# A list scheduler that fixes the order of all operations, with zero-padded keys and natural token order, in a kernel of attention and a dense layer

## The chip, the cores and the metric

One core of one Trainium2 chip. The metric is device time in microseconds (us). The kernel before takes 255.26 us, the median of 2 runs (254.85 to 255.68). All runs below have one core; an execution over 1.5% above the fastest of its kernel is set aside as slow.

Engines are named as in the profile: PE (TensorE matmuls), PEld (TensorE weight loads), DVE (VectorE), ACT (ScalarE), POOL (GpSimd), SP (SyncE, which issues the loads and stores). SBUF and PSUM are the two on-chip memories in which the kernels place their tiles; here every matmul writes to PSUM.

## The reference

Four batches, eight heads, 768 tokens, head size 64. Retrieval heads see the causal half of the scores. Streaming heads see four sink tokens and a window of 64. Which head is which is data. A dense layer with a maximum of two projections follows.

```python
scores = scale * np.matmul(q, k.transpose(0, 1, 3, 2))       # (4, 8, 768, 768)
stream_keep = causal & (is_sink | in_win)                    # n_sink 4, window 64
mask = np.where(is_retrieval_of_head, full_mask, stream_mask)
a = softmax(np.where(mask, scores, -1e9))
x = np.matmul(a, v).transpose(0, 2, 1, 3).reshape(3072, 512)
h1 = x @ w1                                                  # (3072, 1024)
h2 = x @ w2
out = np.maximum(h1, h2) @ w_out                             # (3072, 512)
```

Both kernels use max(h1, h2) = h2 + relu(h1 - h2). So w1 - w2 is prepared once ("wd"), and w2 @ w_out once ("merge", wm). Per token block remain the *up* matmuls (x @ wd, then relu) and the *down* matmuls (x @ wm + relu(...) @ w_out).

## The kernel before

It works through 16 pairs of heads. A pair is loaded, cast to bfloat16 on POOL, transposed on PE, scored, exponentiated on ACT, multiplied by masks on DVE in the near blocks, multiplied by v on PE, and normalised on DVE. The dense work of batch b-1 is sprinkled between the attention steps of batch b by quotas. The framework's scheduler makes the final order.

The two heads of a pair lie one above the other in partitions, so each score matmul uses 64 rows of the array, and the two heads run side by side:

```python
for (j, q0, w, off) in segs:
    for hh in range(2):
        nc.tensor.matmul(sc[hh][:, off:off + w],
            lhsT=kt[64 * hh:64 * hh + 64, j * 128:(j + 1) * 128],
            rhs=qt[64 * hh:64 * hh + 64, q0:q0 + w],
            start=True, stop=True, skip_group_check=True)
```

q and k are loaded in packets of two tokens (512 bytes), which leaves even and odd tokens apart, and the copies after the transposes put them back in order with strides:

```python
in_=src[b, h0:h0 + 2].rearrange("h (m p r) d -> p h m (r d)", p=128, r=2)    # load of q, k
...
o = t.rearrange("q (m p r) -> q m r p", p=128, r=2)
i = psb[:, 0:S].rearrange("q (m r p) -> q m r p", p=128, r=2)
if which == 0: nc.vector.tensor_copy(out=o, in_=i)      # qt
else:          nc.scalar.copy(out=o, in_=i)             # kt
```

All 24 mask tiles are built on DVE before anything else:

```python
for h in range(H):
    for m in range(3):
        nc.vector.scalar_tensor_tensor(out=msk[:, h, m, :], in0=(far0 if m == 0 else far),
            scalar=nsf[:, h:h + 1], in1=causal, op0=ALU.mult, op1=ALU.add)
```

The quota that mixes dense work (`fill`) into attention (`seq`):

```python
quota = total / left / (len(seq) + 2)
...
for si, f in enumerate(seq):
    f()
    ...                      # transposes of the next pair at steps 6 and 8
    spend(quota)             # emits dense steps from fill
```

The softmax here doesn't subtract the row's maximum and nothing guards it: scores larger than these inputs give would overflow.

## Time and profile before

| | before |
|---|---|
| timed, median | 255.26 us |
| span of the profile | 252.9 us |
| PE, DVE, ACT, POOL busy | 84, 59, 50, 22% |
| first score matmul starts | 21.84 us |
| first up matmul starts | 79.89 us |

Lines of the profile page of the kernel before: busy time of each engine (share of the span, instructions), then the span in 40 slices of 6.3 us, each digit the busy share in tenths; PEclk is the granted clock of TensorE.

```profile
PE 212.4 (84%) x1869; PEld 111.9 (44%) x1888; DVE 150.1 (59%) x323; ACT 127.7 (50%) x233; POOL 54.9 (22%) x72
...
PE   0304992649898999999999999999999999999993
...
DVE  6997459864767663675478428546754675370520
ACT  2104880015777675676577666666676667401001
...
PEclk9999999999999999999999999999999999999999
```

PE is at 8 and 9 tenths from the 10th slice (57 us) on, and mostly idle or patchy before that. DVE and ACT are never full for long. The windows view gives the same in us (stretch; length; busy us and instructions of PE, PEld, DVE, ACT, POOL; granted clock; DMA share; GB/s):

```profile
0.00:40.00 40.00, 18.19 (x150) 9.80 (x150) 29.11 (x70) 15.70 (x27) 12.33 (x20) 1.00 1.02 292
40.00:60.00 20.00, 11.31 (x65) 6.48 (x66) 14.70 (x20) 1.96 (x3) 12.65 (x7) 1.00 1.12 243
60.00:100.00 40.00, 37.49 (x388) 20.69 (x390) 25.62 (x55) 27.66 (x53) 9.43 (x14) 1.00 0.44 111
100.00:150.00 50.00, 48.64 (x463) 25.35 (x468) 29.87 (x68) 31.96 (x59) 11.52 (x18) 1.00 0.43 121
150.00:200.00 50.00, 48.45 (x467) 25.29 (x472) 29.15 (x66) 33.42 (x62) 8.95 (x14) 1.00 0.13 44
```

PE is busy 37.5 of 40 us from 60 to 100 us and 97% after that, and the first 60 us hold 29.5 us of PE. So PE binds from 80 us at the latest, where the dense work starts. But "busy" is not "at its peak": a matmul's record runs past the start of the next. The distance from start to start is the better measure. Here is the PE timeline (start us, us, line, operation, output<-inputs, count):

```profile
128.32 0.81 PE L306 MATMUL h<-xt,wd_bf 128*128 128x384 bf16 x4
128.98 0.30 PE L232 MATMUL po<-vb,at 128*128 128x65 bf16 x4
...
130.44 0.81 PE L306 MATMUL h<-xt,wd_bf 128*128 128x384 bf16 x4
131.18 0.39 PE L209 MATMUL sc<-qt,kt 64*128 64x384 bf16 x4
```

Four up matmuls followed by a value matmul take 128.98 - 128.32 = 0.66 us, 165 ns each. Four up matmuls followed by a score take 131.18 - 130.44 = 0.74 us. The median of the interval is 162 ns between up matmuls, and 258 ns from an up matmul to a score: 96 ns are lost where the array changes from 128 to 64 rows.

The chain of waits at the start (start us, us, what):

```profile
5.98 9.44 DVE msk L122 x16
...
16.32 3.86 DVE msk L122 x8
20.18 0.71 DVE bias_94 L126
20.89 0.92 DVE qt L186
...
21.84 1.05 PE sc L209 x6
```

DVE built masks for 14 us, and the copy of the first queries stood behind them in its queue. The first score had to wait for that copy.

### The profile page before, as it was taken

How to read it: one execution, taken by the hardware profiler on the slowest of the kernel's cores; microseconds unless marked ns; L12 is line 12 of the kernel's file. 1: busy time of each engine (PE TensorE's matmuls, PEld its weight loads, DVE VectorE, ACT ScalarE, POOL GpSimd, SP SyncE). 2: the span in 40 equal slices, each digit the busy share in tenths (PEclk: the TensorE clock that was granted, in tenths of full speed). 3: DMA queues.
4: the chain of work that ended last, by engine and by line, in shares of the span. 5: the costliest groups of instructions: out<-in, count | busy, mean ns of one | idle time of the engine just before them, and what ended most of it. 6: DMA issues, size and time to landing. Idle time of an engine off the chain costs nothing.

```text
span 252.9 us, 4818 instructions
## 1 busy us (share of the span) xinstructions
PE 212.4 (84%) x1869; PEld 111.9 (44%) x1888; DVE 150.1 (59%) x323; ACT 127.7 (50%) x233; POOL 54.9 (22%) x72
## 2 busy tenths in 40 slices
PE   0304992649898999999999999999999999999993
PEld 0202551524454644465455545554555464454541
DVE  6997459864767663675478428546754675370520
ACT  2104880015777675676577666666676667401001
POOL 0741119930412213041303121212220100000000
PEclk9999999999999999999999999999999999999999
DMA  5999999993084365535544322012002101111212
GB/s 140 247 268 336 359 399 256 269 254 93 1 189 94 95 166 175 160 89 145 167 106 135 96 81 66 0 44 84 3 0 76 51 3 43 44 41 41 83 44 83
DMA packets 55639, 31.78 MB, mean 126 GB/s; under 512 B 25920, under 2 KB 50496, under 8 KB 55616
## 3 DMA queue, kind: packets, MB, share of 16 engines
q1 hardware_dynamic: 55472, 31.46, 45.4%
q8 instruction: 15, 0.25, 0.4%
q14 instruction: 8, 0.07, 0.1%
q10 hardware_dynamic: 144, 0.01, 0.0%
HBM read 25.17 MB, written 6.29 MB: 124 GB/s over the span
## 4 chain that ended last, share of the span: by engine, by line
PE 67%; DVE 22%; ACT 5%; issue 3%; DMA 2%; ACTq 0%
PE h L306 17%; PE y L320 15%; PE po L232 11%; PE sc L209 9%; DVE msk L122 5%; PE y L317 5%; DVE at L222 4%; PE tp L181 4%; PE wmp L156 3%; DVE x L275 3%; ACT at L218 3%; PE xtp L284 3%; DVE wo_bf L141 2%; DVE w_bf L138 2%; DMA ir_raw<-in_is_retrieval_dram 2%
## 5 line engine op out<-in xcount | busy, mean ns | idle before, releaser
L218 ACT ACTIVATE at<-sc 128x512 bf16<-128x512 f32 (+1 forms) x96 | 48.9, 565 | 24.7 <-PE sc L209 24.5
L222 DVE TENSOR_TENSOR at<-at,msk 128x512 bf16<-128x512 bf16 (+1 forms) x96 | 39.5, 426 | 21.7 <-ACT at L218 21.2
L209 PE MATMUL sc<-qt,kt 64*128 64x256 bf16 (+3 forms) x320 | 42.2, 300 | 10.8 <-DVE qt L186 9.4
L306 PE MATMUL h<-xt,wd_bf 128*128 128x384 bf16 x256 | 50.8, 326 | 0.5 <-ACT ot L323 0.3
L232 PE MATMUL po<-vb,at 128*128 128x65 bf16 x672 | 46.5, 201 | 4.1 <-DVE at L222 2.6
L320 PE MATMUL y<-wo_bf,gt 128*128 128x512 bf16 x190 | 47.7, 379 | 0.1
L232 PEld LDWEIGHTS <-at 128*128 128x128 bf16 x672 | 33.3, 101 | 32.2 <-DVE at L222 15.4
L309 DVE TENSOR_SCALAR gt<-h 128x384 bf16<-128x384 f32 x64 | 35.1, 554 | 20.0 <-PE h L306 18.6
L323 ACT COPY ot<-y 128x512 f32<-128x512 f32 x24 | 14.0, 585 | 54.7 <-PE y L320 54.7
L218 ACT ACTIVATE at<-sc,bias_j 128x512 bf16<-128x512 f32 (+1 forms) x64 | 34.2, 588 | 10.7 <-PE sc L209 10.6
L188 ACT COPY kt<-tp 128x768 bf16<-128x768 bf16 x16 | 16.4, 1026 | 30.7 <-PE tp L181 30.7
L169 POOL CAST qb<-qn 128x768 bf16<-128x768 f32 x16 | 14.1, 883 | 72.4 <-issue 55.4
L306 PEld LDWEIGHTS <-wd_bf 128*128 128x128 bf16 x256 | 22.7, 97 | 15.5 <-issue 3.3
L209 PEld LDWEIGHTS <-kt 64*128 64x128 bf16 x320 | 12.9, 96 | 30.4 <-issue 24.6
L320 PEld LDWEIGHTS <-gt 128*128 128x128 bf16 x192 | 18.0, 98 | 18.4
L317 PE MATMUL y<-wm_bf,xt 128*128 128x512 bf16 x82 | 24.8, 380 | 0.7
L169 POOL CAST kb<-kn 128x768 bf16<-128x768 f32 x16 | 14.2, 888 | 35.5 <-PE tp L181 30.7
L172 POOL CAST vb<-vn 128x768 bf16<-128x768 f32 x16 | 13.8, 863 | 34.4 <-issue 16.7
L218 ACT ACTIVATE at<-sc,bias_94 128x512 bf16<-128x512 f32 x32 | 20.3, 693 | 0.1
L286 DVE COPY xt<-xtp 128x768 bf16<-128x768 bf16 x16 | 8.9, 558 | 18.7 <-PE xtp L284 18.7
L186 DVE COPY qt<-tp 128x768 bf16<-128x768 bf16 x16 | 16.2, 1018 | 3.3 <-PE tp L181 2.9
L181 PE MATMUL tp<-ident,qb 128*128 128x128 bf16 x96 | 9.8, 236 | 9.5 <-POOL qb L169 9.4
(38 smaller groups left out, 140.7 us busy)
## 6 DMA issues: line engine op xcount, KB each, us to landing
qn<-in_q_dram SPq DMA_DIRECT2D x16, 384.0 KB, 6.1
kn<-in_k_dram SPq DMA_DIRECT2D x16, 384.0 KB, 5.3
vn<-in_v_dram SPq DMA_DIRECT2D x16, 384.0 KB, 5.2
out_dram<-ot SPq DMA_DIRECT2D x24, 256.0 KB, 2.0
w_182<-in_moe_w_dram SPq DMA_DIRECT2D x1, 2048.0 KB, 10.3
wo<-in_moe_w_out_dram SPq DMA_DIRECT2D x1, 2048.0 KB, 14.0
w_186<-in_moe_w_dram SPq DMA_DIRECT2D x1, 2048.0 KB, 19.1
ir_raw<-in_is_retrieval_dram ACTq DMA_DIRECT2D x1, 8.0 KB, 4.3
```

Source lines behind the costliest of these rows:

```text
L169: nc.gpsimd.tensor_copy(out=t.rearrange("p n h d -> p h n d"), in_=src.rearrange("p h m (r d) -> p h (m r) d", d=D))
L181: nc.tensor.transpose(psb[:, n * 128:(n + 1) * 128], src[:, n].rearrange("p h d -> p (h d)"), ident)
L186: nc.vector.tensor_copy(out=o, in_=i)
L188: nc.scalar.copy(out=o, in_=i)
L209: nc.tensor.matmul(sc[hh][:, off:off + w], lhsT=kt[64 * hh:64 * hh + 64, j * 128:(j + 1) * 128], rhs=qt[64 * hh:64 * hh + 64, q0:q0 + w], ...
L218: nc.scalar.activation(out=at[:, 0:n], in_=sc[hh][:, 0:n], func=ACT.Exp, scale=scale, bias=bias)
L222: nc.vector.tensor_mul(out=at[:, 0:n], in0=at[:, 0:n], in1=mk)
L232: nc.tensor.matmul(po[hh][:, i * (D + 1):(i + 1) * (D + 1)], lhsT=at[:, off + t * 128:off + (t + 1) * 128], rhs=vb[:, hh, j, :], start=(st ...
L306: nc.tensor.matmul(ps[:, 0:GT], lhsT=wd_bf[:, c, f * 128:(f + 1) * 128], rhs=xts[b][:, c, g * GT:(g + 1) * GT], start=(c == 0), stop=(c == ...
L309: nc.vector.tensor_relu(out=gts[g][:, f, :], in_=ps[:, 0:GT])
L317: nc.tensor.matmul(ps, lhsT=xts[b][:, c, c0:c0 + 128], rhs=wm_bf[:, c, :], start=(c == 0), stop=False)
L320: nc.tensor.matmul(ps, lhsT=gts[g][:, f, t * 128:(t + 1) * 128], rhs=wo_bf[:, f, :], start=False, stop=(f == FC - 1))
```

## The change

Its intent: plan the order of all operations inside the kernel, instead of sprinkling dense work by quotas. Every step becomes an operation with a modelled cost for each engine that may do it, its dependencies, its buffers and a priority. A list scheduler picks, at each step, the operation that can start earliest. This fixes order, engine and buffers. Attention has the lower priority number, so dense work fills what it leaves. Besides:

- each head is scored alone; its keys are padded with 64 zero rows, so every score uses all 128 rows and PE never changes mode;
- q and k come in natural token order, in 256-byte packets, and the copies become plain;
- relu, the output copy and the transposed copies may go to ACT or DVE;
- the mask has two tiles for each head instead of three; weights come in four pieces each; input buffers hold three pairs.

The core of the diff, with cuts:

```diff
+class Plan:
+    def schedule(self):
+        ...
+        while todo:
+            best = None
+            for e, lst in ready.items():          # PE, ACT, DVE, POOL, SP
+                pick = None
+                for o in lst:
+                    t = open_at(o)                # inputs ready and a buffer free
+                    if t is None: continue
+                    s = max(t, clock[e])
+                    key = (s, o.prio) if s > clock[e] + 1e-9 else (clock[e], o.prio)
+                    ...
+            o.engine, o.start, o.end = e, s, s + o.cost[e]
+            ...
+            o.done = o.end + LAT[e]               # PE 0.26, ACT 0.18, DVE 0.17
...
-                nc.tensor.matmul(
-                    sc[hh][:, off:off + w],
-                    lhsT=kt[64 * hh:64 * hh + 64, j * 128:(j + 1) * 128],
-                    rhs=qt[64 * hh:64 * hh + 64, q0:q0 + w],
+                        nc.tensor.matmul(sc.t[:, off:off + w], lhsT=kz.t[:, hh, j * 128:(j + 1) * 128],
+                                         rhs=qt.t[:, q0:q0 + w], ...)
+                o = P.op(score, {"PE": sum(s[2] for s in segs) / 2400 + 0.003 * len(segs)}, tops,
+                         [qt, kz, sc], prio=hr + 0.1 * st)
...
-                out=t, in_=src[b, h0:h0 + 2].rearrange("h (m p r) d -> p h m (r d)", p=128, r=2))
+                out=t.t, in_=src[b, h0:h0 + 2].rearrange("h (n p) d -> p h n d", p=128)),
...
-                nc.vector.tensor_relu(out=gts[g][:, f, :], in_=ps[:, 0:GT])
+                ups.append(P.op(relu, {"DVE": 0.467, "ACT": 0.37}, [o], [bk, gt], prio=15 + b))
...
+    order = P.schedule()
+    with tc.manual_schedule():                    # the framework keeps this order
+        for o in order:
+            o.emit(o.engine)
```

## The prediction

> **What bounds the kernel now.** TensorE. The windows view has PE busy 23.3 to 23.4 of every 24 us from 80 to 200 us and 13.85 of 14 to 214 us; DVE and ACT are near 60% there. Busy is not peak: the starts of successive matmuls in the timeline (80 to 214 us) give 162 ns for an up matmul (128x384), 216 ns for a down matmul (128x512), 56 ns for a transpose, about 29 ns for a value matmul (128x65) at best but 41 ns on average. At the best rates this window's work is about 108 us; it took 134.
>
> The first 80 us are worse: the first score starts at 21.84 us (behind 14 us of mask building in the chain of waits), PE works 2.5 of the first 21 us, and until about 57 us transposes come 107 ns apart, half the later rate, although the page shows the clock granted in full.
>
> **What the change does.**
> 1. Scores. Two heads now run side by side on 64 rows each. Padded, they run one after the other: 86,016 columns at 2.4 per ns is 36 us instead of 18: +18 us of PE.
> 2. No switch of array mode. The Trainium skill (TensorEngine Tiling, Tiling Modes, Key Properties) says that a mode switch drains the array. This trace agrees: up followed by a score takes 258 ns instead of 162, down followed by a score 312 instead of 216. The PE order of before has 200 such switches: 200 x 95 ns = -19 us. So 1 and 2 cancel.
> 3. Startup. The mask no longer delays qt, and the qt/kt copies (1018 and 1026 ns, strided) become plain ones (like xt, 558 ns). All input packets shrink to 256 bytes; at 20 to 22 ns a packet on 16 queues that is about 0.2 MB/us, so q and k of pair 0 land near 6.5 us and the first score starts near 10 us, not 22. Three pairs, the weights and the fourth pair (11 MB) land by about 41 us; dense work of batch 0 starts near 48 us instead of 80.
> 4. Balance. Relu, ot and the copies go to either of ACT and DVE; together they have about 230 us, so neither binds. Attention runs first; the PE order leaves some 68 us of pure dense work for the end, which packs well (97% in before's 214 to 250 us).
>
> **Sum.** PE work at best rates: up 41.5, down 62.2, merge 6.9, transposes 17.9, value 20.5, scores 36.6: 186 us. By 48 us about 28 us of it are done. The middle (90 us of work, static order, three score banks, waits on exp and mask) at about 90% takes 99 us; the dense end takes 70 us; the last copy and store 3 us. 48 + 99 + 70 + 3 = 220 us span; the timed run was 2.4 us over the span. I take a little off for overlap.
>
> **Prediction:** 219 us, 208 to 232. Faster by over 2%: 0.97; within 2%: 0.02; slower: 0.01.
>
> **What would show it.** First score near 10 us; up matmuls from about 48 us; no score followed by a gap of 95 ns; 512-column scores 216 ns apart; ACT and DVE both 50 to 65%; a dense end of about 70 us; transposes 56 ns apart before 57 us.
>
> **What would make it wrong.** PE staying at half rate through the startup (then +8 us); the 256-byte loads starving pair 3 so that the fixed order stalls; waits of value matmuls on masks, since the order is fixed by modelled durations; on the good side, a middle packed above 95% (-6 us).

## The result, and the profile after

The changed kernel takes 223.89 us (223.88 and 223.90, 2 runs). Ratios in this document are the mean time of one kernel's fast runs over that of the other's of the same rounds, so not quite the ratio of the quoted medians: 0.8766 here, 95% interval 0.8727 to 0.8805. That is within the predicted 208 to 232 us, 4.9 us above the point.

| | before | after |
|---|---|---|
| timed, median | 255.26 us | 223.89 us |
| span of the profile | 252.9 us | 221.9 us |
| PE, DVE, ACT, POOL busy | 84, 59, 50, 22% | 90, 55, 68, 22% |
| first score | 21.84 us | 13.60 us |
| first up matmul | 79.89 us | 53.65 us |
| last value matmul | 219.3 us | 146.7 us |

The same lines of the page and of the windows view, for the changed kernel:

```profile
PE 199.0 (90%) x1888; PEld 125.7 (57%) x1888; DVE 122.7 (55%) x298; ACT 151.2 (68%) x291; POOL 48.9 (22%) x59
...
PE   0267986799999999999999999999999999999993
...
DVE  6978999993799888988986876730000000000000
ACT  2158997675988989999989999933527253352721
...
PEclk9999999799999999999999999999999999999999
```

```profile
0.00:40.00 40.00, 23.25 (x284) 16.29 (x284) 36.05 (x86) 24.84 (x45) 14.48 (x22) 1.00 1.07 274
40.00:60.00 20.00, 19.50 (x176) 11.98 (x177) 14.81 (x28) 15.68 (x30) 11.10 (x11) 0.91 1.19 215
60.00:100.00 40.00, 38.70 (x493) 28.18 (x492) 35.69 (x87) 36.85 (x72) 15.56 (x18) 1.00 1.15 228
100.00:150.00 50.00, 49.41 (x585) 34.71 (x584) 36.13 (x100) 44.26 (x89) 7.79 (x9) 1.00 0.24 57
150.00:200.00 50.00, 50.00 (x265) 25.74 (x263) 0.00 (x0) 22.13 (x43) 0.00 (x0) 1.00 0.15 58
```

PE is in use earlier, and the end looks different: DVE has nothing to do after 150 us, and PE is 50.00 of 50 us busy. Attention runs first and leaves 70 us of pure dense work (from 147.6 us, the first down group that starts after the last value matmul). The price stands in the 60 to 100 us line: DVE 35.7 and ACT 36.9 of 40 us, against 25.6 and 27.7 before.

The PE timeline after, answering to the 0.74 us of before:

```profile
88.51 1.02 PE L490 MATMUL mm<-wo_bf,gt 128*128 128x512 bf16 x4
89.37 0.71 PE L398 MATMUL sc<-qt,kz 128*128 128x256 bf16 x4
```

Four down matmuls to a score take 0.86 us, 4 x 215 ns, with no extra step. The medians over the kernel are 162 ns from up to up and 163 ns from up to score.

The chain of waits at the start:

```profile
4.69 7.45 DVE msk L267 x16
...
12.26 0.38 DVE kz L275
...
12.75 0.38 DVE kz L275
...
13.13 0.42 DVE kz L234
```

The masks are still first in the DVE queue, and two zero fills follow. The key copy of pair 0 starts at 13.1 us, although its transposes had ended by 9.6 us.

**A count of useful work.** To compare kernels that use PE differently, I count each matmul at its best interval in the traces: 162 ns up, 216 ns down and merge, 56 ns for a transpose, 29 ns for a value matmul, columns / 2.4 + 2.5 ns for a score, and half of that for a 64-row score, since two run side by side (their starts are 3 to 4 ns apart in the trace of before). This is a derived number. The trace of before lacks about 4 us of it (19 down or merge matmuls are missing from the records).

| useful us of PE in | before | after |
|---|---|---|
| 0 to 20 us | 1.0 | 4.8 |
| 20 to 40 us | 5.2 | 11.2 |
| 40 to 60 us | 4.9 | 17.1 |
| 60 to 80 us | 12.3 | 18.1 |
| 80 to 120 us | 32.3 | 36.3 |
| 120 to 150 us | 23.9 | 29.4 |
| 150 to 190 us | 31.9 | 40.0 |
| total | 162.2 (about 166 with the missing ones) | 184.6 |

The changed kernel has 18 us more to do, and is 31 us shorter. It lost 27 us of PE by 60 us where before lost 49. From 80 to 220 us the kernel before ran at 80 to 81% of the best rate; the changed one ran at 91% from 60 to 120 us and at 98 to 100% from there to 190 us.

### The profile page after: what moved, and what is told of

The parts are those of the page before. It is cut to its first block, busy times and chain, and to the rows that moved or that the text cites. A ratio compares the mean times of both kernels' runs of the same rounds, so it can differ in the third digit from the quotient of the medians.

```text
span 221.9 us, 4796 instructions
## 1 busy us (share of the span) xinstructions
PE 199.0 (90%) x1888; PEld 125.7 (57%) x1888; DVE 122.7 (55%) x298; ACT 151.2 (68%) x291; POOL 48.9 (22%) x59
## 4 chain that ended last, share of the span: by engine, by line
PE 69%; DVE 23%; ACT 3%; issue 2%; DMA 1%; ACTq 0%; DVEq 0%
PE mm L490 18%; PE mm L468 16%; PE sc L398 11%; PE mm L484 9%; PE po L429 7%; DVE at L417 4%; PE mm L326 4%; DVE msk L267 3%; DVE xs L441 3%; PE mm L373 3%; DVE kz L234 3%; DVE at L413 2%; DVE at L421 1%; DMA ir<-in_is_retrieval_dram 1%; PE mm L452 1%
## 5 line engine op out<-in xcount | busy, mean ns | idle before, releaser
L398 PE MATMUL sc<-qt,kz 128*128 128x128 bf16 (+2 forms) x320 | 58.4, 285 | 2.6 <-DVE kz L234 1.8
L490 PE MATMUL mm<-wo_bf,gt 128*128 128x512 bf16 x192 | 46.5, 379 | 0.0
L468 PE MATMUL mm<-xt,wd_bf 128*128 128x384 bf16 x256 | 46.3, 326 | 0.0
L429 PE MATMUL po<-vb,at 128*128 128x65 bf16 x672 | 38.5, 195 | 4.1 <-DVE at L417 1.7
L429 PEld LDWEIGHTS <-at 128*128 128x128 bf16 x672 | 31.8, 98 | 14.5 <-DVE at L417 4.7
L405 ACT ACTIVATE at<-sc,bias_j 128x512 bf16<-128x512 f32 x64 | 38.2, 598 | 2.3 <-PE sc L398 1.9
L398 PEld LDWEIGHTS <-kz 128*128 128x128 bf16 x320 | 28.7, 100 | 16.8 <-issue 2.8
L234 POOL CAST qb<-ld 128x768 bf16<-128x768 f32 x32 | 29.9, 948 | 31.8 <-DMA ld<-in_q_dram 11.5
L468 PEld LDWEIGHTS <-wd_bf 128*128 128x128 bf16 x256 | 23.9, 98 | 14.7
L474 ACT ACTIVATE gt<-mm 128x384 bf16<-128x384 f32 x51 | 25.1, 493 | 5.9 <-PE mm L468 5.6
L373 PE MATMUL mm<-ident,qb 128*128 128x128 bf16 x192 | 17.1, 230 | 11.2 <-POOL qb L234 11.2
L484 PE MATMUL mm<-wm_bf,xt 128*128 128x512 bf16 x96 | 24.6, 379 | 0.0
L405 ACT ACTIVATE at<-sc,bias 128x512 bf16<-128x512 f32 x32 | 22.4, 700 | 1.4 <-PE sc L398 1.2
L417 DVE TENSOR_TENSOR at<-at,msk 128x512 bf16<-128x512 bf16 x32 | 19.2, 600 | 1.5 <-ACT at L405 1.3
L413 DVE TENSOR_TENSOR at<-at,msk 128x512 bf16<-128x512 bf16 x32 | 16.1, 503 | 6.0 <-ACT at L405 5.8
```

The source lines that it names most:

```text
L234: (nc.vector if e == "DVE" else nc.gpsimd).tensor_copy(out=o, in_=i)
L373: nc.tensor.transpose(psb[:, n * 128:(n + 1) * 128], t.t[:, n].rearrange("p h d -> p (h d)"), ident)
L398: nc.tensor.matmul(sc.t[:, off:off + w], lhsT=kz.t[:, hh, j * 128:(j + 1) * 128], rhs=qt.t[:, q0:q0 + w], start=True, stop=True, skip_grou ...
L405: nc.scalar.activation(out=at.t[:, 0:n], in_=sc.t[:, 0:n], func=ACT.Exp, scale=scale, bias=bias)
L413: nc.vector.tensor_mul(out=a, in0=a, in1=m)
L417: nc.vector.tensor_mul(out=a, in0=a, in1=m)
```

## The experiments

Names with b are the kernel before with edits, those with a the changed one. All gave the reference's results, except a_short_cast, which is wrong. "Before" was run again beside each batch: medians 255.57, 254.88, 254.31 and 255.44 us. The changed kernel was not timed again beside them, so kernels are compared through their ratios to before.

### 1. Array mode: a_row64 and b_pad

a_row64 keeps the planned order and its columns, but scores use 64 rows again:

```diff
-lhsT=kz.t[:, hh, j * 128:(j + 1) * 128],               rhs=qt.t[:, q0:q0 + w]
+lhsT=kz.t[64*hh:64*hh + 64, hh, j * 128:(j + 1) * 128], rhs=qt.t[64*hh:64*hh + 64, q0:q0 + w]
```

> The changed kernel with its scores on 64 array rows again, still one head after the other, same planned order, same columns. Theory (a switch of array mode costs about 95 ns of TensorE): the order has 238 changes between scores and other matmuls, so about +20 us, 240 to 247 us; up followed by score about 258 ns instead of 162. Rival (the 95 ns of before were waits for data, or belong to two heads running side by side): within 3 us of 223.9.

Measured: 247.52 us, ratio 0.971 against 0.8766: 23.6 us more in the medians. The PE timeline of a_row64:

```profile
91.64 1.02 PE L490 MATMUL mm<-wo_bf,gt 128*128 128x512 bf16 x4
92.60 0.55 PE L398 MATMUL sc<-qt,kz 64*128 64x384 bf16 x4
```

Four down matmuls followed by a score now take 0.96 us where the changed kernel took 0.86; the median from down to score is 312 ns again, and from up to score 258 ns. So the 96 ns come with the 64-row mode, not with data or with two heads side by side. The rival falls.

The total came close to what I expected, but not all of it for the reason I gave. 170 of the 238 switches lie after the first up matmul, and 170 x 96 ns would be 16 us at most, where part can hide in waits. The first up matmul itself starts at 68.06 us instead of 53.65: 14 of the 26 us that separate the two profiles are lost before it. The clock is a reason. In the trace's clock records TensorE first gets its full clock at 17.5 us in the changed kernel, and only at 58.4 us in a_row64. Before that, transposes come 107 ns apart instead of 56. The PE timeline of a_row64, then of the changed kernel:

```profile
42.38 0.82 PE L373 MATMUL mm<-ident,qb 128*128 128x128 bf16 x6
```

```profile
18.96 0.50 PE L373 MATMUL mm<-ident,qb 128*128 128x128 bf16 x6
```

The one edit was the number of rows, so this too belongs to the 64-row mode. The later first score of a_row64 (15.98 us) doesn't explain it: a_pin and a_port have their first score at 16.0 and 16.1 us, with full-height scores, and their full clock by 21.0 us.

b_pad is the kernel before with padded keys and its own order:

```diff
+kzs = [consts.tile([128, 2, S], BF16, ...) for i in range(2)]   # zeroed once on POOL
-nc.scalar.copy(out=o, in_=i)                                    # kt, one strided copy
+for hh in range(2):                                             # two half copies, ACT and DVE
+    (nc.scalar.copy if hh == 0 else nc.vector.tensor_copy)(out=o_half, in_=i[64*hh:64*hh + 64])
-lhsT=kt[64*hh:64*hh + 64, ...], rhs=qt[64*hh:64*hh + 64, ...]
+lhsT=kt[:, hh, ...],            rhs=qt[:, ...]
```

(Two of the 12 buffers for exponentials had to go for space.)

> The kernel before with zero-padded keys and full-array scores, its order kept (key copy in two halves, one on ACT and one on DVE). Theory of the prediction (padding +18 us and no switches -19 us cancel): 250 to 260 us; up followed by score 162 ns. Rival (padding alone carries a good part of the gain): 245 us or less. Rival (padding costs more than the drains, the gain is all order): 265 us or more.

Measured: 254.94 us, ratio 0.998 (0.9933 to 1.0027). The PE timeline of b_pad:

```profile
127.95 0.81 PE L315 MATMUL h<-xt,wd_bf 128*128 128x384 bf16 x4
128.60 0.60 PE L218 MATMUL sc<-qt,kz 128*128 128x384 bf16 x4
```

The step from up to score is gone (0.65 us), the useful work has grown to 184.6 us, 80 to 214 us run at about 90% instead of 81%, and the time is the same. The prediction's claim that padding and the saved switches cancel holds in the sum. By that sum it need not hold in a kernel with fewer switches or more score columns; that was not run.

### 2. The start: b_mask_late, a_mask_late, a_cheap_mask, a_ld_first

b_mask_late builds the masks of each pair just ahead of it:

```diff
-for h in range(H): ...build three masks...       # before everything
+masks(0); masks(1)                               # after the transposes of pair 0
+if b == 0 and hp + 1 < HP: masks(2 * hp + 2); masks(2 * hp + 3)
```

> The kernel before with the masks of heads 2 to 7 built pair by pair instead of all ahead of the first query copy. Theory (a good part of the gain is the startup): first score near 13 us instead of 21.84, 246 to 251 us. Rival (DVE work and the weights set when the dense work starts, the masks only move): first score earlier but 253 us or more.

Measured: 250.31 us, ratio 0.9805 (0.9734 to 0.9876). The first score starts at 10.43 us instead of 21.84, but the first up matmul at 76.40 instead of 79.89. Of 11 us at the head, about 5 reach the end.

a_mask_late does it in the plan, by priority:

```diff
-prio=h + 0.3                        # masks of head h
+prio=(h if h < 2 else 22.3 + h)
-prio=-40 + 30 * i                   # zero fill of key buffer i
+prio=(-40, 19, 22.2)[i]
```

> The changed kernel with low plan priority for the masks of heads 2 to 7 and for zeroing the later key buffers, so that the first key copy overtakes part of them on DVE. Theory (my missing microseconds were this DVE queue, and DVE is the chain until 35 us): first score near 10.5 us instead of 13.60, 220 to 222 us. Rival (the loads of pair 3 and the weights set the startup): first score earlier, 223 to 225 us.

Measured: 225.21 us, ratio 0.8789: nothing gained; my expectation was wrong. The first score came only 1.3 us earlier (12.27 us), because the cast of the first keys got slower. The POOL timeline of a_mask_late:

```profile
7.74 2.77 POOL L234 CAST qb<-ld 128x768 bf16<-128x768 f32 x1 [0.50 <-DMA ld<-in_k_dram]
```

The usual cast takes 0.83 us; this one took 2.77, while DVE built masks from 7.77 us on. This was the first sign of the collision tested below. And the masks still had to be built on DVE a little later, where DVE was busy too.

The time of the first score in one profile has to be read with care: a_row64 and a_short_cast have the plan of the changed kernel, and theirs came at 15.98 and 15.34 us. Their masks started 0.6 to 0.7 us later (the load of is_retrieval landed at 4.6 to 4.7 us instead of 4.0), and then met more of the casts. The 1.3 us here lie within this scatter.

a_cheap_mask takes the work away instead of moving it. A prepared level tile holds 0 for future tokens, 1 for far ones and 2 for the rest, and each head needs one comparison with a threshold of 0.5 (retrieval) or 1.5 (streaming). One of the 12 buffers for exponentials paid for the tile.

```diff
-for m in range(2): nc.vector.scalar_tensor_tensor(out=msk[:, h, m, :], in0=(far0, far)[m],
-                       scalar=nsf[:, h:h + 1], in1=causal, op0=mult, op1=add)
+nc.vector.tensor_scalar(out=msk[:, h], in0=lev, scalar1=thr[:, h:h + 1], scalar2=None, op0=is_gt)
```

> The changed kernel with masks built by one comparison per head of a prepared level tile against a threshold (correct results; 8 operations with one SBUF input in place of 16 with two). Theory (DVE is the chain of the first 35 us): mask building falls from 7.5 to about 3 us, 220 to 222 us. Rival (loads and weights set the startup, as late masks suggested): within 1 us of the changed kernel.

Measured: 221.57 us, ratio 0.8716 (0.8671 to 0.8761) against 0.8766. The first score starts at 10.56 us and the first up matmul at 51.82. 0.5% of 255 us is 1.3 us; the direction is that of the theory, the size is small, and the intervals of the two ratios overlap. By 40 us its PE has done 19.6 us of useful work, against 16.0. But its profile also lacks a half-clock stretch that the changed kernel's has (41.4 to 44.8 us), so the 1.8 us at the first up matmul can't be put down to the masks alone.

a_ld_first issues the loads of pair 3 ahead of most of the weights:

```diff
-load_weights(3.5)
+pair(0, 0)
+load_weights(4.5)      # weights may start only when pair 0 is cast
```

> The changed kernel with the loads of pair 3 ahead of the weights, plan made anew. Theory (in the startup TensorE starves because v of pair 3 lands behind 6 MB of weights): TensorE does more attention by 40 us, 219 to 222 us. Rival (DVE and ACT are full from 13 to 40 us, whatever lands): within 1.5 us of the changed kernel.

Measured: 231.81 us, ratio 0.911: 8 us worse. My theory was wrong about what the start waits for. The windows view of a_ld_first:

```profile
0.00:40.00 40.00, 24.62 (x302) 17.94 (x303) 33.99 (x88) 26.14 (x49) 14.49 (x24) 1.00 1.10 249
40.00:60.00 20.00, 15.29 (x143) 9.94 (x141) 16.59 (x30) 12.30 (x25) 11.01 (x8) 0.66 1.16 272
```

It does more attention early (17.5 us of useful PE work by 40 us, against 16.0), and then PE has less to do: 15.3 of 20 us busy from 40 to 60 us, at a granted clock of 0.66. In that stretch it does 8.8 us of useful work where the changed kernel does 17.1. The late weights delay the merge and the first up matmul (67.54 us instead of 53.65). Attention was not what lacked early; the dense filler was. The plan said so before the run: it has the first up matmul at 54.6 us, where the plan of the changed kernel has it at 46.3.

### 3. The order: b_all and a_auto, and the choice of engines: a_pin

b_all is the kernel before with the three large parts of the change that need no plan: b_pad and b_mask_late together, and natural token order. (The smaller ones stay as before: three mask tiles, whole weights, four pairs of input buffers, fixed engines.)

```diff
+...b_pad, b_mask_late...
-rearrange("h (m p r) d -> p h m (r d)", p=128, r=2)     # q, k loads: 512-byte packets
+rearrange("h (n p) d -> p h n d", p=128)                # 256-byte packets
-o = t.rearrange("q (m p r) -> q m r p", ...)            # strided copies
+o = t
```

> The kernel before with everything but the planned order: padded keys, natural token order (256-byte input packets, plain copies) and late masks. Theory (the parts other than the order give about what they gave alone, 0 for the padding, -5 for the masks, and 0 to -4 for the plain copies): 246 to 250 us, so that some 23 us of the gain belong to the planned order and its choice of engines. Rival (together they free TensorE, and the plan adds little): 235 us or less.

a_auto is the changed kernel with the same operations, buffers and engines, but the framework's scheduler may move instructions:

```diff
-    with tc.manual_schedule():
-        for o in order:
-            o.emit(o.engine)
+    for o in order:
+        o.emit(o.engine)
```

> The changed kernel, same operations, buffers and engines, but the framework's own scheduler may move instructions instead of keeping the planned order. Theory (the planned order is worth a large part of the gain): 232 us or more. Rival (buffers, choice of engines and full-array scores carry it): within 3 us of the changed kernel.

Measured: b_all 246.08 us, ratio 0.9635 (0.9596 to 0.9674). a_auto 244.06 us, ratio 0.9573 (0.9535 to 0.9611). Each is some 20 us slower than the changed kernel. Keeping the planned order is worth about 20 of the 31 us; everything else in the change gives about 9 to 11. (Natural token order was not run alone. By difference from b_pad and b_mask_late it would have some 4 us of b_all's 9; that assumes that the parts add.)

| useful us of PE in | before | b_all | a_auto | after |
|---|---|---|---|---|
| 0 to 60 us | 11.0 | 19.7 | 25.4 | 33.1 |
| 60 to 80 us | 12.3 | 16.5 | 15.2 | 18.1 |
| 80 to 120 us | 32.3 | 36.8 | 32.5 | 36.3 |
| 120 to 150 us | 23.9 | 28.3 | 24.7 | 29.4 |
| 150 to 190 us | 31.9 | 36.8 | 39.9 | 40.0 |
| first up matmul starts | 79.89 | 72.34 | 63.79 | 53.65 |

The order pays twice. First, it gets dense work started: the first up matmul comes 10 us earlier than in a_auto and 19 us earlier than in b_all. Second, it packs PE while attention and dense work are mixed. The windows view of a_auto shows the second part, from 60 to 150 us:

```profile
60.00:100.00 40.00, 36.54 (x426) 25.41 (x424) 27.53 (x71) 31.25 (x61) 11.94 (x14) 0.97 0.90 178
100.00:150.00 50.00, 46.60 (x574) 33.00 (x572) 37.99 (x101) 44.17 (x85) 14.25 (x16) 1.00 0.37 83
```

Next to the changed kernel's 38.70 and 49.41 us, PE is busy 36.54 and 46.60 us in these stretches. From 60 to 100 us DVE (27.5 against 35.7) and ACT (31.3 against 36.9) are less full as well, so no full engine holds PE back there. Operations, buffers and engines are those of the changed kernel; only the order differs. Part of the time goes through the clock: the records show half clock for 10.2 us in a_auto and 20.5 us in b_all, all between 32 and 63 us, against 3.4 us in the changed kernel. Half of the extra stretch, 3.4 us in a_auto and 8.5 us in b_all, is the most that this can cost (an estimate). Whether the gaps in PE brought the half clock was not tested.

a_pin ties relu and the transposed copy of x to DVE and the output copy to ACT, as before, with the plan made anew:

```diff
-{"DVE": 0.467, "ACT": 0.37}      # relu
+{"DVE": 0.467}
-{"ACT": 0.48, "DVE": 0.6}        # output copy
+{"ACT": 0.48}
-{"DVE": 0.475, "ACT": 0.69}      # transposed x
+{"DVE": 0.475}
```

> The changed kernel with relu and the copy of x transposed tied to DVE, and the output copy tied to ACT, as before; the plan made anew. Theory (free choice of engines matters where ACT or DVE are nearly full, in 53 to 100 us): +2 to +8 us. Rival (neither engine binds, as I predicted): within 2 us of the changed kernel.

Measured: 225.52 us, ratio 0.885 (0.8803 to 0.8898) against 0.8766: about 2 us, just at the border of the two expectations. The free choice is worth little. A version that also tied the copies of q to DVE and of k to ACT could not be built: the planner got stuck.

### 4. What the plan does not know: a_short_cast, a_port, a_slack

The planner gives each operation a start time on its own clock. That is a model and no measurement, but it can be laid beside the trace: how far is PE behind its plan?

| trace time, us | 7 | 48.6 | 62.4 | 81.2 | 101.8 | 120.2 | 147.6 | 211.1 |
|---|---|---|---|---|---|---|---|---|
| behind the plan, us | 1.4 | 7.4 | 8.5 | 9.8 | 11.2 | 13.0 | 13.2 | 13.2 |

After the startup the lag grows as long as POOL casts run. The last cast ends at 126.4 us; from there to the end, including 20 us of attention, it grows by 0.2 us and no more. One case in the changed kernel, POOL first and then DVE (start us, us, ...):

```profile
60.68 0.84 POOL L234 CAST qb<-ld 128x768 bf16<-128x768 f32 x1 [1.06 <-PE sc L398]
```

```profile
60.42 0.41 DVE L413 TENSOR_TENSOR at<-at,msk 128x512 bf16<-128x512 bf16 x1
60.75 1.04 DVE L417 TENSOR_TENSOR at<-at,msk 128x512 bf16<-128x512 bf16 x1
61.83 0.56 DVE L234 COPY kz<-mm 64x768 bf16<-64x768 bf16 x1
```

A mask multiply of 128x512 takes 0.41 us at 60.42. The same operation at 60.75 starts just after a cast and takes 1.04 us; it ends at 61.79, after the cast (61.52). Over the kernel, such multiplies take 419 ns on average when no cast overlaps them (37 of them) and 734 ns when one does (27; the 13 of them at L417 average the 867 ns that an expectation below names). DVE operations that read PSUM are untouched: relu takes 550 ns alone (median) and 550 beside a cast (mean), the copy of q 551 and 553.

The Trainium skill (SBUF — State Buffer, Who interferes with whom) says that DVE and GpSimd share one pair of ports, that a DVE instruction with two SBUF inputs contends with a GpSimd instruction that reads SBUF, and that the loser blocks until the other is done. This trace agrees: the mask multiply and the mask building have two SBUF inputs and are blocked, the PSUM readers are not. Two observations go with it. The loser need not be DVE, nor wait for one instruction only: in a_mask_late the cast recorded from 7.74 us let five mask operations in a row go ahead, and ended at 10.51. And one SBUF input was not safe here: three of the 16 mask comparisons of a_cheap_mask and a_slack took 0.90 to 0.92 us beside a cast, where those that met no cast took about 0.34. Summed over the kernel, DVE operations beside casts took about 12 us longer than their median alone (worked out from the trace).

a_short_cast keeps the planned order and makes the POOL casts short from pair 4 on, so later results are wrong:

```diff
-copy(e, qb, raw)
+copy(e, qb[:, 0:1, 0:1], raw[:, 0:1, 0:1])      # for pairs 4 to 15; same for v
```

> The changed kernel, same planned order, but from pair 4 on the POOL casts of q, k and v convert only one block of 64 columns (results wrong on purpose). Theory (POOL casts block those DVE operations that read two SBUF inputs: 420 ns alone against 867 ns beside a cast, and TensorE falls 5.7 us further behind its plan between 48 and 118 us, exactly while casts run): 217 to 220 us, mask multiplies near 420 ns throughout. Rival (the slip comes from ACT, 92% busy there): within 1 us of the changed kernel.

Measured: the ratio of fast runs is 0.8701 (0.8661 to 0.8741), 1.7 us below the changed kernel; the median of all six runs is 221.55 us. Three of the six (222.07 to 222.43) count as slow by the 1.5% rule; the fast ones are 218.58, 220.65 and 221.03. The profiled run is the 218.58. The second group of 128x512 mask multiplies (line, engine, operation, count, busy us, mean ns, idle before) in the changed kernel and in a_short_cast:

```profile
L417 DVE TENSOR_TENSOR at<-at,msk 128x512 bf16<-128x512 bf16 x32 | 19.2, 600 | 1.5 <-ACT at L405 1.3
```

```profile
L419 DVE TENSOR_TENSOR at<-at,msk 128x512 bf16<-128x512 bf16 x32 | 13.4, 420 | 1.9 <-ACT at L407 1.9
```

600 ns become 420. What TensorE waited for shows the other end of it. Waits from 48 to 118 us in the changed kernel (PEld at L429 is the weight load of a value matmul; who waited, for whom, us in total, times, longest us):

```profile
PEld L429 <- DVE at L417: 2.5, 7, 0.5
PEld L429 <- DVE at L421: 1.5, 4, 0.5
PEld L429 <- DVE at L413: 0.6, 2, 0.4
```

With 0.4 us at L422 that is 4.9 us (from the unrounded waits) for mask multiplies, and none for a cast, so it isn't that the casts themselves came late. In a_short_cast the same view has no wait for a mask multiply. The lag behind the plan grows by 1.7 us from 43.7 to 118 us instead of 5.6 us from 48.6 to 120, and the useful work in 60 to 120 us rises from 54.4 to 57.6 us. So the mechanism is the one named: blocked mask multiplies. The timed gain is less certain: one of the three fast runs lies in the theory's 217 to 220 us, the others between it and the rival, and the intervals of the two ratios overlap. The runs above 220 us have mean clocks of 0.98 to 0.99 instead of 0.999; I can't say how much of the rest that explains.

a_port tells the planner, so that casts and mask multiplies never overlap in the plan. (The edit left out mask building, and in the plan 4 of its 8 operations still overlap casts.)

```diff
-s = max(t, clock[e])
+s = max(t, clock[e], port if o.port else 0.0)    # o.port: casts, wd, mask multiplies
...
+if o.port: port = o.end
```

> The changed kernel with one thing added to the planner: POOL casts and DVE operations with two SBUF inputs never overlap in the plan. Theory (a plan that knows of the collision orders the rest around it): 221 to 223 us. Rival (the lost DVE and POOL time is lost whatever the order): within 1 us of the changed kernel.

Measured: 223.18 us, ratio 0.8763, the same as 0.8766. For the mask multiplies the rival stands: knowing of the collision doesn't help by itself. In the plan no cast overlaps a mask multiply; in the trace of a_port 18 of the 64 multiplies of 512 columns still ran beside one (27 in the changed kernel). The likely reason is that real times differ from planned ones; that was not tested.

a_slack adds slack: cheap masks, the port rule, and a larger modelled latency of DVE, so that each value matmul stands later in PE's order than its mask would need:

```diff
+...a_cheap_mask, a_port...
-LAT = {"PE": 0.26, "ACT": 0.18, "DVE": 0.17, "POOL": 0.2, "SP": 0.0}
+LAT = {"PE": 0.26, "ACT": 0.18, "DVE": 0.4, "POOL": 0.2, "SP": 0.0}
```

> The changed kernel with the cheap masks, the planner that keeps POOL casts and two-input DVE operations apart, and a modelled DVE latency of 0.40 us in place of 0.17, so that TensorE's order leaves each value matmul more slack. Theory (TensorE, which works in order, stalls in 48 to 118 us because the plan leaves no slack for a blocked mask multiply): 217 to 220 us, below every kernel so far. Rival (the slack costs as much as it saves, DVE and ACT being nearly full): 221 to 223 us.

Measured: 217.55 us (216.91 to 217.79, 6 runs), ratio 0.8526 (0.8496 to 0.8556), correct. It beats both kernels: 6 us, 2.7% below the changed one. Its page:

```profile
PE 195.7 (91%) x1888; PEld 125.7 (58%) x1888; DVE 118.2 (55%) x296; ACT 150.3 (70%) x291; POOL 40.8 (19%) x56
...
PE   0398688999989999999999999999999999999993
```

The lag behind the plan is 2.0 us at 47 us and 6.1 at 121 us, where it stops. The slack cost nothing in the plan (PE ends at 204.9 us in it, and at 204.8 in the changed kernel's), and in 48 to 118 us the weight loads of value matmuls waited 0.7 us for mask multiplies instead of 4.9, although 23 of the 64 large multiplies still ran beside a cast. Attention ends at 138.0 us instead of 146.7. All six runs have mean clocks of 0.996 to 1.0. By difference, the slack and the port rule on top of a_cheap_mask gave about 4.8 us (0.8716 to 0.8526); the two were not tried apart in that combination.

## Why the prediction was right, point by point

The measured 223.89 us lies in the range, and the sum was built of the right stages. Its terms, against the profile of the changed kernel (span 221.9 us):

| term | predicted | measured |
|---|---|---|
| until dense work starts | 48 us | 53.65 us |
| middle, attention and dense work mixed | 99 us | 94 us (53.65 to 147.6) |
| dense end | 70 us | 70.4 us (147.6 to 218.0) |
| last copy and store | 3 us | 3.9 us |
| span | 220 us | 221.9 us |
| timed run over span | 2.4 us | 2.0 us |

- **PE binds.** Right, 90% busy after.
- **Padding and saved switches cancel.** Right in the sum: b_pad has ratio 0.998, and a_row64 shows the 96 ns as a matter of the mode. The Trainium skill (TensorEngine Tiling, Tiling Modes) names the drain without a figure. What I did not see is that the half rate of the transposes, which I had noted, came with the 64-row scores: full clock is first recorded at 54 to 60 us with them.
- **Startup, 48 us.** This is the mis-sized step: 53.65 us. "The mask no longer delays qt" held for the queries, which ACT copied at 7.86 us, but the first key copy stood behind all 16 masks and two zero fills on DVE until 13.1 us. So the first score came at 13.60 instead of "near 10". The loads were right: the last weights landed at 41.0 us and v of pair 3 at 42.6 ("by about 41 us"). So was the work ahead of the dense start: 27.6 us ("about 28"). It was done too slowly. By 40 us PE had done 16.0 us of it, where a_slack had done 20.8, with its first score at 10.65, its weights no earlier (42.4 us) and its dense work from 48.54 us on. From 40.3 us to the first up matmul PE is busy without a gap, but from 41.4 to 44.8 us at half clock: 1.8 us of useful work in 3.4 us, so some 1.6 us lost (an estimate).
- **Balance, "neither binds".** Right as a sum: DVE is 55% and ACT 68% busy, and a_pin costs only 2 us. ACT is a little above the predicted 50 to 65%, and the two together are busy for 274 us, not "about 230". But DVE is busy 36 of the first 40 us, and blocked by casts later. I named waits of value matmuls on masks as a risk, but did not know why masks would be late; from 48 to 118 us they came to the 4.9 us of section 4.
- **Middle at 90%.** A little better: 94 instead of 99 us. About half of the difference is packing (it ran at 92%), the other half is work: 86.9 us of useful work stood in it, not 90, because the total is 184.6 us and not 186, and the dense end holds 70 us and not 68. That this offsets the startup is luck.
- **Dense end of 70 us that packs well.** Right: 70.4 us, 100% of the best rate from 150 to 190 us.
- **Half clock through the startup (+8 us if it stayed).** It did not stay: full clock from 17.5 us, and transposes 56 ns apart from 19.0 us on (the first ones after it).
- **The 4.9 us of the miss.** The terms add up to 222.4 us with the launch; I took 3.4 us off "for overlap", and there was none to take. That is most of the miss. The rest is startup +5.7, middle -5, end and stores +1.3, and 0.4 less between span and time.
- **What the prediction did not separate:** it put the earlier dense start down to masks, loads and plain copies. b_all has all three and starts its dense work at 72.34 us, 7.6 us earlier than before and not 32; in time b_mask_late and b_all give 5 and 9 us, and the order gives the other 20. So "48 us instead of 80" came near for reasons that do not carry it, which is luck too: without the planned order it was 72.34, and the prediction doesn't count the order among the causes of the earlier start.

## What to carry to other kernels

If two kinds of work share TensorE, try a planned order before tuning single operations: the same operations took 244 us in the framework's order and 224 in the planned one, and what must be planned first is when the filler (here the weights, then the merge) becomes available. A plan made from modelled durations needs slack at the points where an engine that keeps the planned order waits for an engine whose times vary: 0.23 us more modelled latency, together with cheaper masks and the port rule, was worth 6 us, while the port rule alone was worth nothing. And lay the plan's start times beside the trace's: where the lag grows, something is missing in the model.

## What the Trainium skill lacked or had wrong

- TensorEngine Tiling: it says that a change of tiling mode drains the array, but gives no cost, and promises up to 2x for a contraction of 64 rows. Here a switch cost 96 ns at full clock (162 to 258 ns from up to score, 216 to 312 from down to score), and with 200 switches the 64-row form was no faster than zero padding (ratio 0.998).
- TensorE: Matmul & The Clock Gate (Part 1) says that about 3.4 us of sustained activity releases the half clock, and does not say how matmuls on half of the rows count. In a_row64 full clock was first recorded at 58.4 us, in the changed kernel, whose only difference is full-height scores, at 17.5 us. Over all profiles it is 54.0 to 59.9 us in the three with 64-row scores, and 13.8 to 27.9 us in the eleven with full-height ones. Before those times transposes come 107 ns apart instead of 56. The profile page shows a clock of 9 tenths for that time too, since it has no record yet: read the matmul intervals.
- SBUF — State Buffer: what it says of the shared ports held. It has no such size for this pair of operations: a 128x512 bfloat16 multiply with two SBUF inputs took 419 ns alone and 734 ns on average beside a cast on POOL, and a cast of 0.83 us took 2.77 us against mask building on DVE. It doesn't say that a GpSimd instruction can lose to several DVE instructions in a row, as that cast did to five.
